# Key bits of head 0 thresholded in two pieces, the 256 tokens of the first scores ahead of the other 128

## Chip, cores, metric

One core of one Trainium2 chip. The metric is the device time of one execution in microseconds (us). The profile's span is some 1.8 us shorter than the time. The kernel before: 304.36 us, median of three executions (304.28 to 304.37).

## What is computed

Hash attention, then a feed-forward layer. Only keys that fall in the query's bucket count; the bucket is the sign pattern of six projections.

```python
# q, k, v: (4, 8, 768, 64)   proj: (64, 6)
q_bits = (q @ proj > 0);  k_bits = (k @ proj > 0)         # 6 bits for each token
mask   = bucket(q_bits)[..., :, None] == bucket(k_bits)[..., None, :]
attn   = softmax(where(mask, q @ k.T / 8, -1e9))
x      = heads side by side(attn @ v)                       # (3072, 512)
h      = x @ w_in;  out = (h * cos(h)) @ w_out              # 512 -> 2048 -> 512
```

## The kernel before, as far as it matters

The bits become eight more rows (+0.5 or -0.5) under the 64 rows of q and k, so that one matmul gives the score with the bucket match in it. For head 0, the first, this is done in a hurry at the start. `w` is 0 for queries and 1 for keys, `r` the half of 384 tokens (`HB = 384`, `P = 128`).

```python
def threshold(dst, src):                                  # VectorE, PSUM to SBUF
    nc.vector.tensor_scalar(out=dst, in0=src, scalar1=0.0, scalar2=0.5,
                            op0=ALU.is_gt, op1=ALU.subtract)

def place_direct(hd, w, r, jp):
    held["bits", hd % NE] = hd
    threshold(e_rows(hd, D, KEXT, r)[:, w],
              jp[64 * w + 32 * r:64 * w + 32 * r + BR, 0:HB])

def scores(s, u):                                         # one unit = 512 columns
    ...                                                   # u = 0: 384 columns of key block 0, 128 of block 1
    nc.tensor.matmul(out=st[:, o:o + n], lhsT=e[:, 1, jt * P:(jt + 1) * P],
                     rhs=e[:, 0, t0 * P + c:t0 * P + c + n], start=True, stop=True)
    ...
    nc.scalar.activation(out=pts[s][:, u * UNIT:(u + 1) * UNIT], in_=st, func=ACTF.Exp, ...)

# the start, in program order; each engine works through its own part of it in this order
    ...
        transpose(0, 0, "act")                            # TensorE, copy out by ScalarE
        ...
        transpose(0, 1)                                   # copy out by VectorE
        jq = hash_direct(0, 0)                            # TensorE, fp32: query bits before the sign
        jk = hash_direct(0, 1)                            # the same for the keys
        cast(0, 0, "act", slice(0, 1))
        place_direct(0, 0, 0, jq)
        cast(0, 0, "act", slice(1, 2))
        place_direct(0, 1, 0, jk)
        cast(0, 1, "act")
        place_direct(0, 1, 1, jk)
        place_direct(0, 0, 1, jq)
        transpose(1, 0, "act", ps_o, "o_att")
        transpose(1, 1, "act", ps_o, "o_att")
        scores(0, 0)
        hash_group([1])                                   # bit projection of head 1
        scores(0, 1)
    ...
```

The softmax here doesn't subtract the row's maximum and nothing guards it: scores larger than these inputs give would overflow.

## Time and profile before

| | share of the span of 302.7 us |
|---|---|
| TensorE (PE) busy | 98% |
| ScalarE (ACT) busy | 81% |
| VectorE (DVE) busy | 63% |
| chain that ended last | PE 92%, ACT 7%, DVE a rounded 0% |
| stretch that the change touches | 6.9 to 9.5 us |

Head 1's transposes begin at 6.75 us, and the second exponential, from which the chain runs on, begins at 9.45 us: 2.70 us. The lines themselves are quoted in the prediction.

### The profile page before, as it was taken

The numbers are of one execution on the slowest core, as the hardware profiler recorded it, in microseconds if no ns is written. First come the engines' busy times: TensorE is split into PE (matmuls) and PEld (weight loads), VectorE is DVE, ScalarE is ACT, GpSimd is POOL, SyncE is SP. The second block draws the span as 40 slices with busy tenths as digits, with TensorE's granted clock in tenths as the row PEclk, the third lists the DMA queues.
The fourth block names the chain that finished last, engine by engine and source line by source line (L and its number), as shares of the span: only waits on it lengthen the run. The fifth ranks groups of instructions, "written<-read, shape, count | busy, mean of one in ns | idle before, by whom it ended". The sixth has DMA issues, their size and how long they took to land.

```text
span 302.7 us, 7140 instructions
## 1 busy us (share of the span) xinstructions
PE 298.1 (98%) x2813; PEld 183.4 (61%) x2813; DVE 190.9 (63%) x385; ACT 244.7 (81%) x461; POOL 123.7 (41%) x134
## 2 busy tenths in 40 slices
PE   8999999999999999999999999999999999999995
PEld 3677776656555665666565656666656665654544
DVE  3998948966688887678856676539832364230730
ACT  5879998979988998997787978998778896842821
POOL 4796986899696896407914530000000000000000
PEclk9999999999999999999999999999999999999999
DMA  7689999966959986449025362440001300023002
GB/s 223 237 136 288 246 204 175 314 130 131 245 180 226 206 184 161 89 111 339 3 87 148 83 92 74 89 92 1 2 19 52 88 2 35 37 55 104 35 37 69
DMA packets 52993, 38.06 MB, mean 126 GB/s; under 512 B 32896, under 2 KB 48736, under 8 KB 52960
## 3 DMA queue, kind: packets, MB, share of 16 engines
q1 hardware_dynamic: 44416, 27.05, 36.1%
q0 software_dynamic: 8320, 10.49, 16.3%
q8 instruction: 22, 0.36, 0.5%
q14 instruction: 11, 0.09, 0.1%
q10 hardware_dynamic: 224, 0.07, 0.1%
HBM read 27.27 MB, written 6.29 MB: 111 GB/s over the span
## 4 chain that ended last, share of the span: by engine, by line
PE 92%; ACT 7%; issue 0%; DVE 0%; ACTq 0%
PE y L511 24%; PE st L330 19%; PE st L487 14%; PE o_att L373 11%; PE o_att L487 10%; ACT pt L338 7%; PE tp L487 4%; PE tp L236 3%; PE tp L511 2%; PE y L141 1%; PE y L186 1%; PE y L693 1%; PE tp L254 1%; PE tp L186 0%; PE tp L301 0%; ACT o_sb L522 0%
## 5 line engine op out<-in xcount | busy, mean ns | idle before, releaser
L338 ACT ACTIVATE pt<-st 128x512 f16<-128x512 f32 x288 | 154.2, 622 | 19.8 <-PE st L330 18.7
L511 PE MATMUL y<-wout,gt 128*128 128x512 f16 (+1 forms) x384 | 111.2, 365 | 0.0
L330 PE MATMUL st<-ext 72*128 72x512 bf16 (+3 forms) x480 | 108.1, 294 | 0.5 <-ACT pt L338 0.2
L373 PEld LDWEIGHTS <-pt 128*128 128x128 f16 x1152 | 71.2, 97 | 27.8
L373 PE MATMUL o_att<-v_ext,pt 128*128 128x65 f16 x1152 | 82.3, 193 | 0.0
L487 PEld LDWEIGHTS <-win 128*128 128x128 f16 x512 | 50.1, 98 | 32.7
L207 POOL TENSOR_SCALAR blk<-nat_qk 128x768 bf16<-128x768 f32 x23 | 50.0, 2172 | 35.4 <-DMA nat_qk<-in_k_dram 19.6
L330 PEld LDWEIGHTS <-ext 72*128 72x128 bf16 x480 | 43.9, 97 | 29.6 <-issue 7.0
L487 PE MATMUL st<-xT,win 128*128 128x384 f16 x256 | 48.5, 326 | 0.0
L511 PEld LDWEIGHTS <-gt 128*128 128x128 f16 x416 | 35.5, 98 | 12.5
L499 DVE TENSOR_TENSOR gt<-o_att,cs 128x384 f16<-128x384 f32 x46 | 25.5, 555 | 24.9 <-ACT cs L495 22.8
L487 PE MATMUL o_att<-xT,win 128*128 128x384 f16 x184 | 37.4, 326 | 0.0
L499 DVE TENSOR_TENSOR gt<-st,cs 128x384 f16<-128x384 f32 x64 | 34.5, 553 | 3.0
L495 ACT ACTIVATE cs<-st 128x384 f16<-128x384 f32 x64 | 30.7, 491 | 5.8 <-PE st L487 5.4
L407 DVE TENSOR_TENSOR osum<-o_att,flat 128x390 f32<-128x390 f32 x24 | 13.6, 565 | 33.1 <-PE o_att L373 32.5
L522 ACT COPY o_sb<-y 128x512 f32<-128x512 f32 (+1 forms) x24 | 13.4, 557 | 15.8 <-PE y L511 15.8
L495 ACT ACTIVATE cs<-o_att 128x384 f16<-128x384 f32 x46 | 22.6, 491 | 4.3 <-PE o_att L487 4.1
L226 DVE STREAM_TRANSPOSE qk<-nat_qk 128x768 f32<-128x768 f32 x24 | 23.0, 967 | 0.3
L127 POOL TENSOR_TENSOR vacc<-nat_v 128x384 f32<-128x384 f32 x16 | 17.2, 1073 | 0.0
L424 DVE TENSOR_TENSOR xtok<-osum,rec 128x384 f16<-128x384 f32 x24 | 16.0, 668 | 0.9
L122 POOL CAST v_ext<-nat_v 128x768 f16<-128x768 f32 x16 | 13.3, 828 | 4.3 <-PE o_att L373 2.7
L487 PE MATMUL tp<-xT,win 128*128 128x384 f16 x72 | 14.6, 326 | 0.0
(82 smaller groups left out, 217.3 us busy)
## 6 DMA issues: line engine op xcount, KB each, us to landing
out_dram<-o_sb SPq DMA_DIRECT2D x23, 256.0 KB
nat_qk<-in_q_dram SPq DMA_DIRECT2D x10, 384.0 KB
nat_qk<-in_k_dram SPq DMA_DIRECT2D x10, 384.0 KB
nat_v<-in_v_dram SPq DMA_DIRECT2D x10, 384.0 KB
nat_v<-in_v_dram POOLq DMA_DIRECT2D x6, 384.0 KB, 8.5
win<-in_moe_w_in_dram POOLq DMA_DIRECT2D x8, 256.0 KB, 9.1
wout<-in_moe_w_out_dram POOLq DMA_DIRECT2D x8, 256.0 KB, 8.3
nat_qk<-in_q_dram POOLq DMA_DIRECT2D x5, 384.0 KB, 8.6
```

The costliest lines, as they stand in the source:

```text
L127: nc.gpsimd.tensor_add(acc, x[:, :, 0:3 * D], x[:, :, 3 * D:6 * D])
L207: engine.tensor_scalar(out=blk[hd].rearrange("p t w d -> p w t d"), in0=nat[hd].rearrange("p w (t d) -> p w t d", d=D), scalar1=QK_PRESCAL ...
L226: nc.vector.transpose(out=f32[hd].rearrange("p w c -> p (w c)"), in_=nat[hd].rearrange("p w c -> p (w c)"),)
L330: nc.tensor.matmul(out=st[:, o:o + n], lhsT=e[:, 1, jt * P:(jt + 1) * P], rhs=e[:, 0, t0 * P + c:t0 * P + c + n], start=True, stop=True,)
L338: nc.scalar.activation(out=pts[s][:, u * UNIT:(u + 1) * UNIT], in_=st, func=ACTF.Exp, bias=EXP_BIAS, scale=EXP_SCALE,)
L373: nc.tensor.matmul(out=o_state[s][:, qt * VW:(qt + 1) * VW], lhsT=pts[s][:, f:f + P], rhs=v_all[:, hd % NV, token(hd // H, jt)], start=(i ...
L407: nc.vector.tensor_tensor(out=both.rearrange("p (n t) d -> p n t d", n=n), in0=o_ps[:, 0:SB].rearrange("p (n t) d -> p n t d", n=n), in1=f ...
L424: nc.vector.tensor_tensor(out=xtok[b][:, t0:t0 + nt, h * D:(h + n) * D].rearrange("p t (n d) -> p n t d", n=n), in0=o_ps[:, :, 0:D].rearra ...
L487: nc.tensor.matmul(out=hp[:, 0:TOK], lhsT=win_t[ft][:, ff * P // WC, ff * P % WC:ff * P % WC + P], rhs=xT[b, c][:, ft], start=(ft == 0), s ...
L495: nc.scalar.activation(out=cs, in_=hp[:, 0:TOK], func=ACTF.Sin, bias=math.pi / 2.0, scale=1.0)
L499: nc.vector.tensor_tensor(out=gt, in0=hp[:, 0:TOK], in1=cs, op=ALU.mult)
L511: nc.tensor.matmul(out=y_state[b, t][:, cut], lhsT=gates[b, c][ff][:, tt * P:(tt + 1) * P], rhs=wout_t[:, ff, cut], start=(ff == 0), stop= ...
```

## The change

The first unit of scores needs the bits of keys 0 to 255 only, but waits for the threshold of 384. The change cuts that threshold in two, so that the scores can start once the first 256 are done.

```diff
-    def place_direct(hd, w, r, jp):
+    def place_direct(hd, w, r, jp, cut=slice(0, HB)):
         held["bits", hd % NE] = hd
         threshold(
-            e_rows(hd, D, KEXT, r)[:, w],
-            jp[64 * w + 32 * r:64 * w + 32 * r + BR, 0:HB],
+            e_rows(hd, D, KEXT, r)[:, w, cut],
+            jp[64 * w + 32 * r:64 * w + 32 * r + BR, cut],
         )
@@
         cast(0, 0, "act", slice(1, 2))
-        place_direct(0, 1, 0, jk)
+        place_direct(0, 1, 0, jk, slice(0, 2 * P))
         cast(0, 1, "act")
+        place_direct(0, 1, 0, jk, slice(2 * P, HB))
         place_direct(0, 1, 1, jk)
```

## The prediction

> **What bounds the kernel now.** I read four views, in this order: the page's summary and its chain that ended last; that same chain in order of time for the first 14 us, because the changed code runs once, at the start; the instructions of each engine in order of time from 4 to 10.6 us; and the durations of the threshold's line, L176, and of the score matmuls' line, L330.
>
> ```profile
> span 302.7 us, 7140 instructions
> PE 298.1 (98%) x2813; PEld 183.4 (61%) x2813; DVE 190.9 (63%) x385; ACT 244.7 (81%) x461; POOL 123.7 (41%) x134
> ...
> PE 92%; ACT 7%; issue 0%; DVE 0%; ACTq 0%
> ```
>
> The end of the kernel is set by TensorE (PE), with ScalarE (ACT) for 7% of the chain. VectorE (DVE), whose work is changed, has a rounded share of 0% of it. A change on DVE counts only if it lets PE or ACT start something earlier that the chain then follows. So the question is about one stretch of about 2 us, and the chain through it is this:
>
> ```profile
> 6.82 0.81 PE o_att L141 x6
> 7.63 0.34 PE st L330 x2
> 7.97 1.12 PE y L186 x4
> 9.09 0.34 PE st L330 x2
> 9.42 0.02 issue
> 9.45 2.63 ACT pt L338 x5
> ```
>
> Columns: start in us, length, engine, tile, line, count. L141 is the pair of transposes of head 1, the first L330 is the first unit of scores (the one that the change is meant to release), L186 is the bit projection of head 1, the second L330 is the second unit of scores, and from 9.45 the exponentials run. At first sight the first unit of scores is on the chain. But these pieces are joined by modelled ends, so I looked at who released each of them. First PE's weight loads, which come just ahead of their matmuls, with the idle time before them in brackets:
>
> ```profile
> 6.75 0.64 PEld L141 LDWEIGHTS o_att<-ident,nat_qk 128*128 128x128 f32 x6 [1.15 <-issue]
> 7.56 0.13 PEld L330 LDWEIGHTS <-ext 72*128 72x128 bf16 x2 [0.17 <-issue]
> 7.90 0.14 PEld L186 LDWEIGHTS y<-qk,projx 128*32 128x32 f32 x2 [0.21 <-ACT qk L150]
> 8.25 0.14 PEld L186 LDWEIGHTS y<-qk,projx 128*32 128x32 f32 x2 [0.22 <-ACT qk L150]
> 9.01 0.11 PEld L330 LDWEIGHTS <-ext 72*128 72x128 bf16 x2 [0.62 <-issue]
> ```
>
> Then ACT and DVE in the same stretch:
>
> ```profile
> 7.34 0.86 ACT L150 COPY qk<-o_att 128x384 f32<-128x384 f32 x2 [0.47 <-PE o_att L141]
> 8.09 0.61 ACT L338 ACTIVATE pt<-st 128x512 f16<-128x512 f32 x1
> 9.45 1.64 ACT L338 ACTIVATE pt<-st 128x512 f16<-128x512 f32 x3 [0.74 <-PE st L330]
> ...
> 6.31 0.55 DVE L176 TENSOR_SCALAR ext<-tp 8x384 bf16<-8x384 f32 x1 [0.86 <-PE tp L301]
> 6.89 1.15 DVE L176 TENSOR_SCALAR ext<-y 8x384 bf16<-8x384 f32 x2
> 8.05 0.55 DVE L176 TENSOR_SCALAR ext<-tp 8x384 bf16<-8x384 f32 x1
> 9.12 0.55 DVE L176 TENSOR_SCALAR bits<-y 64x384 bf16<-64x384 f32 x1 [0.52 <-PE y L186]
> ```
>
> The reader is to see three things. (1) There is a wait to remove: the key threshold runs from 6.89 to about 7.45, and the first score weights are loaded at 7.56, 0.17 us after the last load of the transposes ended (6.75 + 0.64 = 7.39). (2) The next PE work, the projection of head 1, is not released by the scores. It waits for ACT's copies (L150) of head 1's transposes, twice: 0.21 us ending at 7.90, 0.22 us ending at 8.25. (3) The exponential that reads the first unit starts at 8.09 with no idle time in front of it: it sits directly behind ACT's second copy.
>
> **What the Trainium skill says.** "VectorE: DVE Perf Modes", section "The TRN2 errata — SBUF-src ops pay a fixed extra latency per instruction": a DVE instruction costs about one cycle per element of its free size, at 0.96 GHz, plus a fixed part measured at about 150 cycles. For 384 columns that is 534/0.96 = 556 ns, for 192 it is 356 ns. The trace agrees:
>
> ```profile
> L176 DVE TENSOR_SCALAR ext<-y x2: 555/558/561, 6.9 to 7.5; 8x384 bf16<-8x384 f32 x2
> ...
> L176 DVE TENSOR_SCALAR bits<-tp x7: 358/549/559, 37.4 to 186.2; 128x384 bf16<-128x384 f32 x5, 128x192 bf16<-128x192 f32 x2
> ```
>
> The same page, section "Two Vector instructions with no wait between them": an instruction starts only when the earlier ones have finished if its operands start in another quadrant of 32 partitions, and otherwise sooner. The four thresholds of head 0 read partitions 0, 64, 96 and 32, so all are held. The trace agrees: they start at 6.31, 6.89, 7.47, 8.05, that is 0.58 apart for 0.55 of duration, while two L152 copies of the same width that both start at partition 0 come at 11.12 and 11.59, only 0.47 apart. "Perfetto Trace Analysis", section "Identifying Dependency Chains": instructions that wait for several engines can get a semaphore instruction of their own in front. The trace has one of 51 ns on PE's queue at 7.5 for L330. The same page, "Tensor Engine Instruction (MATMUL, LD_WEIGHTS)": matmul ends are estimated, not observed; hence I use starts and releases here.
>
> **The change part by part.** *Key bits in two pieces.* The first unit of scores has 512 columns: 384 of key block 0 and 128 of key block 1. It needs the bits of keys 0 to 255, which is the new first piece. The second unit needs block 2 as well, the new second piece. Slope from the two L176 sizes: (558 - 358)/(384 - 192) = 1.04 ns per column. Piece of 256: 558 - 128 x 1.04 = 425 ns. Piece of 128: 558 - 256 x 1.04 = 292 ns.
>
> *First piece.* It still starts at 6.89 (released by its predecessor) and ends at 6.89 + 0.425 = 7.31 or 7.32, instead of 7.45: 0.13 us earlier. The weight load came 0.11 us after the threshold's end (7.56 - 7.45), so it could come at 7.43. PE allows about that: the last transpose starts at 7.36 and they start 0.11 apart, so PE takes the next at about 7.47. The first score matmuls then start near 7.48 instead of 7.59: about 0.1 us earlier.
>
> *What becomes of that 0.1 us.* Score matmuls of 384 and 128 columns started at 7.59 and 7.75 and were out of PE's way before 7.90; then PE idled for ACT's copy. That copy ends at 7.34 + 0.48 = 7.82 and hangs on the transposes, which lie ahead of the scores on PE and never saw the threshold. So the projection still starts at 7.90, its second half at 8.25, and the second unit of scores at 9.01. The first exponential is held at 8.09 by ACT's copies. Gain on the path: 0.
>
> *Second piece.* It reads and writes the quadrants of the first piece, so it is not held and starts 0.11 us before the first ends (0.58 - 0.47 from the two pitches above): about 7.21, ending near 7.50. The third threshold (other input quadrant) is held and starts at about 7.53 instead of 7.47. Cost on DVE: about 0.06 us if not held, (425 + 292 - 558) + 30 ns of gap = 0.19 us if it is held. The fourth then ends at 8.66 to 8.79 instead of 8.60. DVE was idle for 0.52 us before its next work at 9.12, so nothing reaches it. The buffer of the query bits, next written by transposes whose weights load at 9.14, is free 0.35 us before. The second unit of scores (9.01) finds the second piece long done. The third threshold's bits (ending at 8.09 to 8.22) are first used by the third unit, whose weights load at about 9.47. Cost on the path: 0.
>
> *Waits.* The second unit of scores gets a new semaphore condition for the second piece. If it takes an instruction of its own, that is 51 ns at a place where PE's queue is waiting for the projection anyway; at worst 0.05 us.
>
> Sum: 304.36 + 0 (first piece) + 0 (DVE time in its gap) + 0 to 0.05 (wait), and a possible few hundredths less if modelled ends hide a real tie. I put the time at 304.35.
>
> **The rivals.** *The gain arrives.* The chain draws the first scores (7.63) directly in front of the projection (7.97), and if the projection started when the scores leave PE, up to 0.1 us would be passed on, giving 304.26. Against it: the load at 7.90 shows idle time ending with ACT's copy, and again at 8.25; even with the first half earlier, the second half is tied to 8.25. *DVE becomes late.* If the added instruction cost far more than 0.19 us, the projection's threshold at 9.12 would slip, and with it the transfer of head 1's bits (PE waits 0.62 us for that at 13.41): each tenth past the gap of 0.52 us would cost a tenth. It would need an added 0.5 us, some 9 tenths of a full threshold; then 304.4 to 304.7. *The wait is moved.* The score load could have been waiting for ACT's cast rather than for DVE. ACT's casts ended at 5.48 + 1.39 = 6.87, so no; and it would make the same 0.
>
> **Range and chances.** Every mechanism is smaller than 0.2 us, or 0.07%. The three runs of before span 0.09 us and the profiled run was at 304.44, so the range is mostly spread of runs and of chips: 304.12 to 304.56. A move of 2% would be 6.1 us, more than the entire stretch touched; 0.5% on each side covers only what I can't see.
>
> **What would show it.** In the changed profile: two thresholds ext<-y of about 425 and 292 ns followed by one of 558; the first L330 weight load near 7.45 instead of 7.56; L186's loads still at 7.90 and 8.25 behind ACT qk L150; the first exponential still at 8.09, the second at 9.45; the bits<-y threshold at 9.12 with its idle time down to 0.3 to 0.5 us. It would be wrong if the second exponential leaves 9.45 by more than 0.05 us, or if the L186 loads move with the scores.

## The result

The changed kernel took 304.80 us (median of six executions, 304.16 to 305.84). The kernel before was run beside it again; with the three executions above its median is 304.37, but it now ranged from 304.28 to 305.58. The ratio is 1.0008, with a 95% interval of 0.9984 to 1.0032: the same within what can be told. (Ratios here are the mean time of one kernel's fast runs over that of the other's of the same rounds, so not quite the ratio of the medians.) The median lies 0.24 us above the predicted range.

In the profile, the changed stretch did as predicted, but all of it came 0.1 us later. First the chain of waits of the changed kernel from head 1's transposes on (start, length, what):

```profile
6.92 0.81 PE o_att L141 x6
7.73 0.22 PE st L330 x2
7.95 0.02 issue
7.97 1.21 PE y L186 x4
```

Before, the first scores filled the gap up to the projection of head 1 (L186); now they end earlier and a gap of 0.02 us "issue" is left in front of the projection. The time saved has become waiting. Next, the instructions of PE's weight loads, of ACT and of DVE in order of time, changed kernel (a line with x3 merges three instructions that follow each other and shows the shape of the first; the L176 line at 6.97 holds both pieces and the third threshold):

```profile
6.85 0.64 PEld L141 LDWEIGHTS o_att<-ident,nat_qk 128*128 128x128 f32 x6 [1.16 <-issue]
6.97 1.22 DVE L176 TENSOR_SCALAR ext<-y 8x256 bf16<-8x256 f32 x3
7.43 0.86 ACT L150 COPY qk<-o_att 128x384 f32<-128x384 f32 x2 [0.48 <-PE o_att L141]
7.51 0.15 PEld L330 LDWEIGHTS <-ext 72*128 72x128 bf16 x2
7.96 0.14 PEld L186 LDWEIGHTS y<-qk,projx 128*32 128x32 f32 x2 [0.30 <-ACT qk L150]
8.18 0.61 ACT L338 ACTIVATE pt<-st 128x512 f16<-128x512 f32 x1
8.35 0.14 PEld L186 LDWEIGHTS y<-qk,projx 128*32 128x32 f32 x2 [0.24 <-ACT qk L150]
9.22 0.55 DVE L176 TENSOR_SCALAR bits<-y 64x384 bf16<-64x384 f32 x1 [0.46 <-PE y L186]
9.54 1.64 ACT L338 ACTIVATE pt<-st 128x512 f16<-128x512 f32 x3 [0.74 <-PE st L330]
```

The three thresholds in that line, with their durations (min/median/max in ns):

```profile
L176 DVE TENSOR_SCALAR ext<-y x3: 278/422/561, 7.0 to 7.6; 8x256 bf16<-8x256 f32 x1, 8x128 bf16<-8x128 f32 x1, 8x384 bf16<-8x384 f32 x1
```

Counted from the start of head 1's transposes (6.75 before, 6.85 now):

| | before | changed |
|---|---|---|
| first score weights (L330) | 0.81 | 0.66 |
| idle before them | 0.17 | none |
| head 1's projection, first half (L186) | 1.15 | 1.11 |
| idle of the weight loads before it, ended by ACT's copy | 0.21 | 0.30 |
| its second half | 1.50 | 1.50 |
| first exponential | 1.34 | 1.33 |
| second exponential | 2.70 | 2.69 |

The wait of 0.17 us is gone, the first scores are 0.15 us earlier, and the next wait, for ScalarE's copies, has grown by 0.09 us. The second exponential has not moved.

So nothing at this place explains the 0.43 us between the two medians, and the profiled execution of the changed kernel was in fact a fast one (304.16 us, span 302.4). Two questions stay: is the slack of the first scores really the reason, and where does the rest come from?

### The profile page after: what moved, and what is told of

It reads as the page before. It is cut to its first block, busy times and chain, and to the rows that moved or that the text cites. A ratio compares the mean times of both kernels' runs of the same rounds, so it can differ in the third digit from the quotient of the medians.

```text
span 302.4 us, 7141 instructions
## 1 busy us (share of the span) xinstructions
PE 297.7 (98%) x2813; PEld 183.4 (61%) x2813; DVE 189.5 (63%) x386; ACT 244.7 (81%) x461; POOL 123.7 (41%) x134
## 4 chain that ended last, share of the span: by engine, by line
PE 91%; ACT 7%; DMA 1%; issue 0%; ACTq 0%
PE y L511 24%; PE st L330 19%; PE st L487 14%; PE o_att L373 11%; PE o_att L487 10%; ACT pt L338 7%; PE tp L487 4%; PE tp L236 2%; PE tp L511 2%; PE y L141 1%; PE y L186 1%; DMA nat_qk<-in_q_dram 1%; PE tp L254 1%; PE tp L186 0%; PE tp L301 0%; ACT o_sb L522 0%
## 5 line engine op out<-in xcount | busy, mean ns | idle before, releaser
L330 PE MATMUL st<-ext 72*128 72x512 bf16 (+3 forms) x480 | 108.1, 294 | 0.5 <-ACT pt L338 0.2
L207 POOL TENSOR_SCALAR blk<-nat_qk 128x768 bf16<-128x768 f32 x23 | 50.1, 2178 | 34.8 <-DMA nat_qk<-in_k_dram 19.8
L330 PEld LDWEIGHTS <-ext 72*128 72x128 bf16 x480 | 44.0, 97 | 29.4 <-issue 6.9
L522 ACT COPY o_sb<-y 128x512 f32<-128x512 f32 (+1 forms) x24 | 13.4, 557 | 15.8 <-PE y L511 15.8
```

Source lines behind the costliest of these rows:

```text
L207: engine.tensor_scalar(out=blk[hd].rearrange("p t w d -> p w t d"), in0=nat[hd].rearrange("p w (t d) -> p w t d", d=D), scalar1=QK_PRESCAL ...
```

## The experiments

Theory A: the first scores have slack behind ScalarE's copies, DVE's added 0.1 us lies in a gap, the change moves nothing that the end follows, and the spread belongs to the machine and the kernel, not to the change. The rivals are in the expectations. All outputs are right. Executions over 1.5% above the fastest of the same kernel (309.06, 309.26 and 311.11 us) are slow ones and left out.

### Both kernels again

**aa_before**: no edit, the kernel before timed against itself.

> The kernel before under another name, timed against itself. Theory A (the change moves nothing that the end follows, and the spread of the result, 304.16 to 305.84, belongs to the machine): ratio 1.000, and these identical programs spread as widely as the changed kernel did, some 1 to 1.5 us from lowest to highest, in both columns. Theory B (the change made the time uneven): all runs here lie within 0.3 us, 304.2 to 304.5.

Measured: 304.10 to 305.21 in one column and 304.00 to 305.62 in the other, ratio 1.0002 (0.9978 to 1.0025). Identical programs spread by 1.6 us on one chip. The 0.09 us of the first three executions, on which the range had been built, was luck. Theory B falls.

**after_again**: no edit.

> The changed kernel once more, beside the kernel before. Theory A: ratio within 0.999 to 1.001, the same spread as the kernel before has on this chip; in the trace the first score weights again 0.1 us nearer to the transposes, the projection of head 1 and the second exponential not moved against them. Theory B: median 0.3 us or more above the kernel before, and a wider spread.

Measured: 303.85 to 305.62, ratio 1.0003 (0.9977 to 1.0028). First score weights 0.66 us and second exponential 2.69 us after the transposes began, as in the first profile of the change.

### How much slack the first scores have

**key_late**, on the kernel before:

```diff
-        place_direct(0, 1, 0, jk)
-        cast(0, 1, "act")
         place_direct(0, 1, 1, jk)
+        cast(0, 1, "act")
+        place_direct(0, 1, 0, jk)
```

> The kernel before with the thresholds of the two key halves in the other order on VectorE, so that the first scores wait about 0.58 us longer. Read in the trace, from the first transposes of head 1 to the second exponential (2.70 us before, 9.45 - 6.75). Theory A, the first scores have slack, because the second half of head 1's projection waits for ScalarE's copy until 8.25 whatever they do (some 0.45 us of slack, as the two halves can run side by side): the second exponential comes 0.1 to 0.25 us later. Rival C, the chain as drawn, scores directly ahead of the projection: 0.5 to 0.58 us later. Time in both too small to tell from the spread (within 0.3%).

PE's weight loads and ACT of key_late in order of time:

```profile
6.18 0.64 PEld L141 LDWEIGHTS o_att<-ident,nat_qk 128*128 128x128 f32 x6 [0.65 <-issue]
7.54 0.13 PEld L330 LDWEIGHTS <-ext 72*128 72x128 bf16 x2 [0.73 <-ACT qk L150]
7.88 0.14 PEld L186 LDWEIGHTS y<-qk,projx 128*32 128x32 f32 x4 [0.21 <-ACT qk L150]
9.08 1.15 ACT L338 ACTIVATE pt<-st 128x512 f16<-128x512 f32 x2 [0.50 <-PE st L330]
```

The first score weights come 1.36 us after the transposes' start instead of 0.81, 0.55 us late, and the second exponential 2.90 instead of 2.70: 0.20 us late. The other 0.35 us was slack. The third line shows how: the four weight loads of the projection now come in one go, because both copies are there by then; in the kernel before they came in two pairs, each behind its copy. Rival C (0.5 us or more) falls. (The profile names ACT as the releaser of L330; by their times it was the later threshold on DVE.) The time, 304.32 to 305.25 us, tells nothing.

Two executions of the unedited kernel before, made later (before_look2 and before_look4 below), show the same without an edit. In them the first score weights came 1.04 and 1.01 us after the transposes' start instead of 0.81, behind 0.40 and 0.37 us of idle time, and the second exponential was still at 2.69 and 2.70.

### How much slack VectorE has

**dve_dose**, on the changed kernel:

```diff
         place_direct(0, 0, 1, jq)
+        place_direct(0, 0, 1, jq)
+        place_direct(0, 0, 1, jq)
```

> The changed kernel with the last threshold of head 0 done three times, 1.15 us more of VectorE work in the gap that the second piece eats from (0.46 us idle left in the changed kernel). Theory A: the bits of head 1 come 0.6 to 0.8 us later, the second exponential is not moved; so an added piece of 0.1 us is far from hurting. Rival D, VectorE has no real slack there: the second exponential is 0.3 us or more later too.

The second exponential came at 8.64 us, 2.69 after the transposes' start at 5.95: not moved. Head 1's bits started 3.23 us after that instead of 2.37, 0.86 later, a little more than expected (in this execution the thresholds as a whole began 0.12 us later against the transposes). But the dose was not free, and by another way than either theory had named; the weight loads of dve_dose:

```profile
9.21 0.31 PEld L141 LDWEIGHTS tp<-ident,nat_qk 128*128 128x128 f32 x3 [0.88 <-DVE ext L176]
```

The transposes of head 2 write the PSUM buffer that held the query bits, and had to wait 0.88 us until VectorE had read it. Counted from the start of head 1's transposes, the last threshold of head 0 ended at 3.20 us instead of 1.91 (the first profile of the change), 1.30 later, and the weights of head 2's transposes came at 3.26 instead of 2.39, 0.87 later. So some 0.42 us was slack. That agrees with the traces: in the first profile of the change VectorE was done with this buffer 0.48 us ahead of these weights, in dve_dose 0.05 us. (The prediction read off 0.35 us for a held second piece; not held, as it turned out, the same reading gives 9.14 - 8.66 = 0.48.) The change keeps clear of it by about 0.4 us. The times (304.78 to 305.02 us and one of 307.94; ratio 1.0032, 0.9991 to 1.0074) tell nothing here.

### Taking away what hides the wait

**pair_first_whole** and **pair_first_pieces** put head 1's transposes ahead of the key projection and head 1's projection ahead of the first scores, with the threshold whole and in pieces (lines left out are marked ...):

```diff
         jq = hash_direct(0, 0)
-        jk = hash_direct(0, 1)
         cast(0, 0, "act", slice(0, 1))
-        place_direct(0, 0, 0, jq)
         cast(0, 0, "act", slice(1, 2))
-        ...
+        transpose(1, 0, "act", ps_o, "o_att")
+        transpose(1, 1, "act", ps_o, "o_att")
+        jk = hash_direct(0, 1)
+        place_direct(0, 0, 0, jq)
+        place_direct(0, 0, 1, jq)
+        cast(0, 1, "act")
+        place_direct(0, 1, 0, jk)              # _pieces: the two pieces instead
+        place_direct(0, 1, 1, jk)
+        hash_group([1])
+        scores(0, 0)
         scores(0, 1)
```

> Without the change, but with head 1's transposes and their copies ahead of the key bit projection of head 0, both query thresholds of head 0 early, and the projection of head 1 ahead of the first scores. This takes away what the first scores were hidden behind in another way: TensorE no longer waits for ScalarE's copies. Theory A: from the start of head 0's key copy on VectorE to the second exponential 3.6 to 4.2 us where TensorE is at full rate in time (4.05 and 4.10 in the two kernels of before's order that were), 0.3 us or more less than before in the like state. Of that up to 0.4 us nothing that can be told from the spread reaches the end (ratio 0.998 to 1.001), since early gains were given back at transfers by 98 us. Rival E: a start that is 0.4 us shorter ends 0.4 us earlier (ratio about 0.9987).

> The same with the key bits in two pieces, as in the change. Theory A: head 1's projection keeps TensorE until the whole threshold would be done as well, so the first score weights come right behind it in both, and the pieces move the second exponential by less than 0.05 us against pair_first_whole in the like state of the clock; ratio within 0.001 of it. Rival C: 0.1 us earlier.

The expected length of the start was missed in both. Head 1's data is not there so early: the transposes waited for its load, for queries until 6.06 us in pair_first_whole, and for keys until 7.04 us in pair_first_pieces. From head 0's key copy to the second exponential it took 4.40 and 5.00 us, not 3.6 to 4.2, so the order gains nothing. One part of theory A held: the first score weights came right behind head 1's projection, 0.78 and 0.76 us after the first load of its second half, against 0.76 (9.01 - 8.25) for the second scores of the kernel before, although the profile names VectorE as what they waited for. Ratios 0.9998 (0.9975 to 1.0021) and 1.0008 (0.9987 to 1.0030). The two differ in when data arrived, and so in how long the projection covers the threshold; they don't compare the pieces with the whole.

**pair_scores_whole** and **pair_scores_pieces** are the same with the first scores back ahead of the projection:

```diff
-        hash_group([1])
         scores(0, 0)
+        hash_group([1])
         scores(0, 1)
```

> As pair_first_whole, but the first scores stay ahead of head 1's projection, whose inputs are ready by then: nothing hides the key threshold any more. Theory A: the first score weights wait for it and come 0.1 us after its end, so from the start of the key threshold to the first exponential it is about 1.1 us, and the projection of head 1 follows the scores without a wait for ScalarE. Later at the second exponential than pair_first_whole by 0.1 to 0.3 us.

> The same with the pieces. Theory A: here the cut pays as it was meant to: from the start of the key threshold to the first exponential, and to the projection of head 1, 0.10 to 0.15 us less than in pair_scores_whole. If it pays nothing here either, the slack of the first scores was not the reason. In the time nothing to be told from the spread.

The key threshold, the first score weights and the first exponential, in order of time, first of pair_scores_whole:

```profile
7.75 1.15 DVE L176 TENSOR_SCALAR ext<-y 8x384 bf16<-8x384 f32 x2 [0.42 <-PE y L301]
8.42 0.13 PEld L330 LDWEIGHTS <-ext 72*128 72x128 bf16 x2 [1.44 <-ACT ext L168]
8.87 0.60 ACT L338 ACTIVATE pt<-st 128x512 f16<-128x512 f32 x1 [0.48 <-PE st L330]
```

and of pair_scores_pieces:

```profile
7.27 1.22 DVE L176 TENSOR_SCALAR ext<-y 8x256 bf16<-8x256 f32 x3 [0.53 <-PE y L301]
7.81 0.13 PEld L330 LDWEIGHTS <-ext 72*128 72x128 bf16 x2 [1.30 <-ACT qk L150]
8.26 0.60 ACT L338 ACTIVATE pt<-st 128x512 f16<-128x512 f32 x1 [0.40 <-PE st L330]
```

From the threshold's start to the weights it is 0.67 against 0.54 us, to the first exponential 1.12 against 0.99. The projection, which here follows the scores, starts 1.01 against 0.88 us after, and the second exponential 2.21 against 2.08. The cut is worth 0.13 us at every one of these, as expected: the same cut pays once nothing else is being waited for. This is the strongest evidence that the slack, and not some cost of the cut, took the gain away. One expectation missed: pair_scores_whole was to be 0.1 to 0.3 us later at the second exponential than pair_first_whole, and from head 0's key copy it was 0.76 us later (5.16 against 4.40). It is one profile of each kind, so the 0.13 us rests on the two traces agreeing with the difference of the two thresholds, 555 and 422 ns. The order itself is no better than before (ratios 1.0017, 0.9989 to 1.0046, and 0.9999, 0.9976 to 1.0022).

### Where the spread comes from

**before_look1, after_look1, before_look2, after_look2**, and then **before_look3, after_look3, before_look4, after_look4**: no edit, eight profiled executions on one chip.

> One more profiled execution of the kernel before, for the source of the spread. Theory S: it comes from where TensorE's clock turns to full rate (4.2 to 6.8 us so far) and from transfers: the start of head 1's transposes is within 0.2 us of 6.75 where the clock turned after 6 us and 0.4 us or more earlier where it turned before 5.3 us; further steps of 0.2 to 0.6 us against the first profile lie at waits on loads or moved bits near 61 us and 92 to 98 us, and at no place where the two kernels differ. Rival T: the offset against the first profile grows slowly everywhere, as with a slower clock.

> One more profiled execution of the changed kernel. Theory S as for before_look1; between the end of head 1's transposes and the second exponential no difference over 0.05 us from the kernel before in the like state of the clock; first score weights 0.10 to 0.15 us after the last weights of the transposes, instead of 0.17 and more after them in the kernel before.

> A second profiled execution of the kernel before: the same as for before_look1 by theory S, steps at the clock's turn and at waits on transfers; by rival T a slow drift.

> A second profiled execution of the changed kernel: the same as for after_look1 by theory S; by rival T a slow drift.

> A third profiled look at the kernel before. Theory S: the difference of its time from the first profile (304.44 us) is within 0.15 us of the offset that TensorE's last instructions show against that profile, and this offset comes in steps at the clock's turn (5 to 7 us), at the wait for head 1's bits (13.4 us), at the bit projection near 37 and 61 us and at 92 to 98 us. An execution of 305 us or more shows larger steps at the same places. Rival T: time outside the span, or drift.

> A third profiled look at the changed kernel; theory S and rival T as for before_look3: steps at the known waits that add up to the difference in time, none between the first scores and the second exponential over 0.05 us in the like state of the clock.

> A fourth profiled look at the kernel before; theory S and rival T as for before_look3, with the same numbers.

> A fourth profiled look at the changed kernel; theory S and rival T as for after_look3, with the same numbers.

For the table, the start of each matmul on TensorE was paired with that of the same matmul in the first profile of the kernel before, and the median offset taken in four stretches. The two kernels have the same TensorE program, so this works for both. Columns: time less 304.44 us; when TensorE's clock turned to full rate, by the trace's own record of it; offsets, all in us.

| execution | time | clock turned | 9 to 12 | 14 to 18 | 39 to 58 | from 190 |
|---|---|---|---|---|---|---|
| before_look1 | -0.45 | 6.82 | 0.15 | 0.15 | 0.13 | -0.44 |
| before_look2 | -0.70 | 6.00 | -0.29 | -0.13 | -0.24 | -0.71 |
| before_look3 | 0.28 | 4.48 | -0.51 | 0.51 | 0.92 | 0.28 |
| before_look4 | -0.60 | 6.17 | -0.19 | -0.18 | -0.20 | -0.63 |
| aa_before | -0.05 | 5.20 | -0.47 | -0.35 | -0.49 | -0.07 |
| first profile of the change | -0.28 | 6.67 | 0.09 | 0.09 | 0.08 | -0.28 |
| after_again | -0.51 | 6.83 | 0.12 | 0.13 | 0.11 | -0.51 |
| after_look1 | 0.08 | 6.83 | 0.10 | 0.10 | 0.07 | 0.08 |
| after_look2 | 0.09 | 4.43 | -0.63 | 0.02 | 0.20 | 0.09 |
| after_look3 | 0.15 | 4.45 | -0.15 | 0.93 | 0.75 | 0.15 |
| after_look4 | 0.31 | 7.16 | 0.29 | 0.30 | 0.83 | 0.28 |

The last column equals the time to 0.03 us in every row, so the account is closed: the differences arise in steps at a few places and hardly drift in between. Theory S holds in this, T falls. Not all its marks were met: the first score weights came 0.02 us after the transposes' last weights in after_look1 (0.10 to 0.15 expected) and 0.15 in before_look1 and before_look3 (0.17 and more), and in after_look4 the transposes began 0.24 us from 6.75 (0.2). Four places can be named; what is said of the cause at the last two is read off the traces, and no run tested it. A fifth, between 90 and 99 us, moved some executions by up to 0.33 us and was not followed up.

*The clock.* If TensorE turns to full rate early, the key projection of head 0 (L301) runs faster. Its four passes in the first profile of before, where the clock turned at 6.56 us (min/median/max in ns):

```profile
L301 PE MATMUL y<-qk,projx x4: 714/763/809, 5.5 to 6.1; 128*8 128x384 f32 x4
```

and in aa_before, where it turned at 5.20 us:

```profile
L301 PE MATMUL y<-qk,projx x4: 486/488/492, 5.5 to 5.8; 128*8 128x384 f32 x4
```

In the runs that keep the order of the two kernels, head 1's transposes, which come behind it, begin between 5.95 us (dve_dose, turned at 4.17) and 6.99 us (after_look4, turned at 7.16). The Trainium skill has this in "TensorE: Matmul & The Clock Gate", section "Part 1: The HAM clock gate (the "warmup" mystery)": TensorE starts at half rate, and activity is judged in free-running windows of about 3.4 us, so that the moment of the turn varies by execution. This case agrees: 4.1 to 7.2 us in twenty profiled executions, and the record of the full rate lasts either 296.96 or 300.37 us in all of them, 3.41 us apart. This alone is several times the gain that the change was after.

*The transfer of head 1's bits.* An early start is mostly given back at 13.4 us, where the scores of head 1 wait for their bits. In after_look3, the weight load that waited:

```profile
14.34 0.11 PEld L330 LDWEIGHTS <-ext 72*128 72x128 bf16 x2 [1.80 <-DMA ext<-bits]
```

In the first profile of before the same load came at 13.41 after 0.62 us of idle, which was the projection ahead of it and no wait: the matmuls show no gap there, and the same 0.62 stands ahead of the second scores at 9.01. The three executions of the table whose clock turned before 5 us all met this wait for more than a microsecond, among them after_look2, whose head start of 0.63 us was gone by 14 us. TensorE waited here in seven of the fourteen profiles of the two kernels; in those a gain at the second exponential would have ended at this point.

*A port shared by VectorE and GpSimd*, near 33 us. In the last run of the change, after_more (below), VectorE's scaling of head 8 (L207) and GpSimd beside it, then the bit projection that waited:

```profile
33.02 2.32 DVE L207 TENSOR_SCALAR blk<-nat_qk 128x768 bf16<-128x768 f32 x1
33.11 0.84 POOL L122 CAST v_ext<-nat_v 128x768 f16<-128x768 f32 x1
33.90 1.01 POOL L127 TENSOR_TENSOR vacc<-nat_v 128x384 f32<-128x384 f32 x1
37.14 0.47 PEld L254 LDWEIGHTS tp<-qk,projb 128*32 128x32 f32 x12 [0.71 <-DVE qk L226]
```

and the same pair in before_look1:

```profile
33.48 0.59 DVE L207 TENSOR_SCALAR blk<-nat_qk 128x768 bf16<-128x768 f32 x1
33.54 1.39 POOL L127 TENSOR_TENSOR vacc<-nat_v 128x384 f32<-128x384 f32 x1
```

One and the same VectorE instruction takes 0.59 us or 2.32. In before_look1 it was GpSimd's instruction beside it that was lengthened instead (1.39 against 1.01). "SBUF — State Buffer", section "🔬 SBUF: two separate sides", says that VectorE in a two-port mode and GpSimd share a port pair as an exclusive lock, held for a whole instruction, and that the other is blocked meanwhile. These lines agree: the long one ends at 35.34, which is 0.43 us after the second GpSimd instruction; and L207's 0.59 us is 0.77 ns per column, less than the 1.04 of the thresholds, as fits a faster mode. No run took GpSimd's work away here, so the lock is a reading and not tested. What decides which of the two is held is open: in after_more VectorE's recorded start is 0.09 us ahead of GpSimd's, and VectorE was held. A small shift can become half a microsecond here: in after_look4 an offset of 0.30 us ahead of this place was 0.83 us behind it. That TensorE waits here for a late VectorE was seen in eight of the twenty profiles, for 0.17 to 0.71 us; of the seven profiles of each of the two kernels, in three of the changed one and one of the kernel before, too few to tell apart.

*The bit projection near 61 us* (L236) waits for VectorE in the same way: 0.54 us in the first profile of before, none in before_look1. Ahead of it stand VectorE's copies L276: their first pair took 0.63 to 1.32 us, and in the seven of the twenty profiles in which it took 1.24 us or more, and in no other, TensorE waited 0.54 us or more. Presumably the copies are long for the same lock; that was not tested.

No execution of 305 us or more of the two kernels was caught with a profile. The slower ones among the profiled runs are variants (305.06 and 305.26), and they close on the same places.

### Is there a small real cost?

In the eight looks the changed kernel lay at 304.52 to 304.75 and the kernel before at 303.74 to 304.72. So two last runs: **after_more** and **before_more**, no edit.

> The changed kernel, five rounds. Theory A, no cost beyond the spread: mean of its fast runs within 0.25 us of the kernel before's (ratio 0.9992 to 1.0008). Rival F, a real cost of about 0.5 us: ratio 1.0012 or more, and clearly above that of before_more.

> The kernel before against itself once more, five rounds: ratio 0.9992 to 1.0008 by both theories; how far it misses 1.000 is how far after_more may miss it by chance.

Measured: 1.0017 (0.9998 to 1.0035) for the change and 0.9993 (0.9977 to 1.0009) for the kernel before against itself. Theory A's band for the first is missed, rival F's is met in the value, but the interval takes in both, and the control shows a chance deviation of half that size. Over all executions of the result and of the two jobs in which both kernels were timed in five rounds, the changed kernel has a mean of 304.94 us (18) and the kernel before 304.64 us (39); the difference, 0.29 us, has a standard error of 0.17 us, from their standard deviations of 0.63 and 0.48 us. The sum leaves out the eight looks. All four groups point the same way, the changed kernel's mean being higher by 0.23 us (the result), 0.12 (first job), 0.52 (the looks) and 0.51 (last job); compared within each group and then taken together, that is 0.33 us with a standard error of 0.14. This leans towards a cost of about a third of a microsecond, 0.1% of the time, without showing one, and no experiment here names a cause for it. If there is one, the traces say that it is not where the code was changed: the second exponential came 2.69 to 2.75 us after the start of head 1's transposes in the changed kernel (six profiles) and 2.69 to 2.73 in the kernel before (six), leaving out one profile of each in which the transposes themselves waited for head 1's load.

## Why the prediction was wrong, point by point

The mechanism was right at the place that was changed. What failed is the term of the sum that stands for the kernel itself: its base of 304.36 us and the spread put around it.

- **What bounds the kernel**: right. The chain through the stretch is head 1's transposes, ScalarE's copies, head 1's projection, second scores.
- **First piece**: right. 422 ns measured for 425, and the scores 0.15 us earlier (their matmuls 0.13) for "about 0.1".
- **"Gain on the path: 0"**: right, 2.69 against 2.70 us, and its reason was tested twice: delayed scores cost only a part of their delay (key_late), and the same cut pays 0.13 us where nothing hides it (pair_scores). This is shown as far as the second exponential; whether the whole kernel has a cost of some 0.3 us elsewhere is open (above). The slack was even larger than said, as the two halves of the projection can run together.
- **Second piece**: right. 278 ns for 292; not held, since it began at 7.32 before the first ended at 7.39; the third threshold came 0.66 us after the first piece began instead of 0.58, for 0.06 us expected. Idle before head 1's bits 0.46 us, in the stated 0.3 to 0.5. Durations: the Trainium skill's 150 cycles, which the prediction takes from "VectorE: DVE Perf Modes", are measured there on an instruction that reads SBUF; see the last section.
- **New wait**: no cost. No third semaphore instruction stands ahead of the early score matmuls.
- **"Range and chances"**: this is the step that failed. The prediction said that "the range is mostly spread of runs and of chips", and sized that spread from 0.09 us between three executions and one profiled run at 304.44. The kernel before, run again in all these jobs, gave 303.69 to 305.95 with a standard deviation of 0.5 us. Its base was low too: the mean of these executions is 304.64 us, not 304.36, which alone lies above the range's upper end of 304.56. Medians of six, drawn at random from the 39 executions of the kernel before that were counted above, fall outside the range in about half of the draws (48%), so the range would often have failed even if the change did nothing. Of the 0.59 us between the changed kernel's mean of 304.94 and the predicted 304.35, the base makes 0.28; the other 0.3 is chance or a real cost. (The text's "0.5% on each side" does not fit its own range, which is 0.07% on each side.)
- **"PE waits 0.62 us for that at 13.41"**: misread. The 0.62 us is the time of the projection ahead of the load, as at 9.01; TensorE did not wait there in that profile.
- **"What would show it"**: the marks at fixed times (7.90, 9.45 moved by no more than 0.05) were badly made. The second exponential was at 9.54 because everything from the first load on was 0.1 us later; as intervals from the transposes the marks would have held.

One trace could have warned of a part of it: TensorE was still at half rate in the key projection (passes of 763 ns), so the start depends on when the clock turns. That the VectorE instruction near 33 us (L207, 1.40 us there) varies from 0.55 to 2.32 us only further executions could show.

## What to carry to other kernels

Before shortening a wait, look at what the *next* instruction of the same engine waits for; if another engine releases that one, the gain turns into idle time there, and delaying the wait in an experiment measures the slack directly. Quote a range from the kernel's own spread over many executions: three that agree to 0.1 us are no measure of it, and where a time hangs on a clock that turns at a varying moment or on two engines that hold each other up, effects of a tenth of a microsecond can be seen only in intervals of a trace. A closed account of offsets between two traces shows where a difference really arises, which here was not where the code differs.

## What the Trainium skill lacked or had wrong

- "TensorE: Matmul & The Clock Gate" (Part 1) gives the turn to full rate as varying by about 500 ns either way between runs of one program; here, with the first matmul at 0.92 us each time, it came from 4.14 to 7.16 us in twenty executions, a range of 3 us, which fits the page's own free-running window of 3.4 us better than its 500 ns.
- "VectorE: DVE Perf Modes" (errata section): its fixed part of about 150 cycles would make the piece of 128 columns 290 ns; 278 was measured. For 256 and 384 columns it holds (422 and 548 to 562 ns), though the page measured it with SBUF as the source, and the thresholds read PSUM, for which its table has 120 cycles (258, 392 and 525 ns, too short for all three).
- "SBUF — State Buffer" has the exclusive lock, and that the one which starts first gets it, but not that the waiting side can be passed over by a second instruction in a row, as the trace of after_more reads if the lock is the cause: a VectorE instruction of 0.55 to 0.59 us, when not held, took 2.32 us, past two GpSimd instructions, though its recorded start was 0.09 us ahead of the first of them.
- No page gives how long a small transfer may take while loads are under way: in the seven profiles of the two kernels in which TensorE waited for head 1's bits, they were sent at 9.1 to 9.5 us and awaited until 13.1 to 14.3 us.
